# A range clamp moved from VectorE to GpSimd, and a maximum over four written as three elementwise maxima

## The chip, the cores and the metric

The kernel runs on one core of a Trainium2 chip. The core has five engines, each with its own queue of instructions that it takes in order: TensorE (PE; its weight loads are PEld) for matrix products, VectorE (DVE), ScalarE (ACT), GpSimd (POOL), and SyncE (SP), which starts most transfers. They meet only at semaphores. The metric is the device time of one execution in microseconds. Three runs of the kernel before took 1162.79, 1162.80 and 1165.26 us, a median of 1162.8 us.

## The reference, cut to what matters

Three blocks follow each other: an attention with 32 memory slots per head, a dense layer with three weight matrices, and an 8-expert layer in which each expert takes a fixed number of tokens by descending logit.

```python
a = np.exp(phi - np.max(phi, axis=2, keepdims=True))      # phi: 8 x 8 x 576 x 32
a = a / (np.sum(a, axis=2, keepdims=True) + 1e-09)
k_m, v_m = einsum('bhsm,bhsd->bhmd', a, k), einsum('bhsm,bhsd->bhmd', a, v)
attn = softmax((q @ k_m.T) / 8)                            # 8 = sqrt(head_dim)
x = (attn @ v_m) as 4608 tokens x 512
h = np.maximum(np.maximum(x @ w1, x @ w2), x @ w3)         # 512 -> 768
x = h @ w_out                                              # 768 -> 512
logits = x @ w_gate                                        # greedy choice, 576 tokens per expert
out[mask] = np.maximum(x[mask] @ m_w1[e], 0) @ m_w2[e]     # for each expert e
```

The dense weights w1, w2, w3 and w_out arrive as float64. The change touches their conversion to float32 and the maximum over the 576 tokens of phi.

## The kernel before, in words

The eight batches are handled as four units of two. For unit 0 the order of all work is written out as one string of steps, ORDER (lines 30 to 70); later units are interleaved by a planner (Flow) that spreads attention steps between the matrix products of the unit before. In ORDER a name is a step, an exclamation mark continues a step at its next `yield`, and a leading 1 means unit 1. `s0` is the maximum over tokens, `c.0` to `c.11` are the conversions of the layer-1 weights (six column chunks by two row halves), `d.0` to `d.5` those of w_out, `f` folds weights into the attention values, `L` is layer 1 and `s6` the softmax's division.

`s0` (line 270) takes one batch of phi as a tile of 128 partitions, in which a partition holds 4 tokens of each of 8 heads by 32 slots. It reduces the four to one (line 273), adds the remaining 64 tokens by a maximum over 64 partitions (line 276), and TensorE then transposes the result for the maximum over partitions. It runs twice per unit: twice at the start, for unit 1 in lines 35 and 44 of ORDER, and later for units 2 and 3.

`conv` (line 519) turns a float64 tile into float32 by its integer words. ScalarE writes the absolute value of the high word, read as a float32, into the destination (line 529). VectorE clamps that to the range LEAST to MOST (line 532), shifts it by three bits (line 533), brings in the sign (line 535) and the top bits of the low word (line 536). Tiles are 128x768 for the layer-1 weights and 128x512 for w_out. The layer-1 result is also stored to a scratch tensor (line 538), and the next weights are requested. In ORDER `c.n` is the absolute value and `c!.n` all the rest.

GpSimd's own work in the first 160 us is four additions per batch (lines 312 to 315), the softmax's division (line 437), half of the subtractions that split folded weights into a high and a low part (line 586) and the same for w_out (line 547). The low parts feed layer 1 (line 602), whose first matrix product for each chunk and batch half needs them.

Of the kernel before, what the change touches and what calls it, by code (L numbers as in the profile page):

```python
# [12 lines left out]
OP = mybir.AluOpType  # L13
AX = mybir.AxisListType
# [56 lines left out]
LEAST, MOST = 2.0 ** -15, 122879.9921875  # L71
# [71 lines left out]
def moe_kernel(tc, q, k, v, phi, w1, w2, w3, w_out, w_gate, m_w1, m_w2, out):  # L143
    nc = tc.nc
    PE, V, A, G, SP = nc.tensor, nc.vector, nc.scalar, nc.gpsimd, nc.sync
    B, H, S, D = q.shape
# [13 lines left out]
    with ExitStack() as ctx:  # L160
# [106 lines left out]
        def att_steps(u):  # L267
            steps = []

            def s0(b):  # L270
                ph, phr = st["ph", u, b], st["phr", u]
                mt = lp.tile([128, H * M], F32, name="mt", bufs=1)
                V.tensor_reduce(mt.rearrange("p (h m) -> p h m", h=H), ph.rearrange("p h i m -> p h m i"),
                                axis=AX.X, op=OP.max)
                r = slice(64 * b, 64 * b + 64)
                V.tensor_tensor(mt[r], mt[r], phr[r].rearrange("p h m -> p (h m)"), op=OP.max)
                st["mt", u, b] = mt
# [165 lines left out]
            if u < 2:  # L443
                return dict(s0=s0, t0=s0b, s1=s1, t1=s1b, r=s2s, s2=s2, s3=s3, s4=s4, s5=s5, s6=s6)
            add(3.0, P(s0, 0))
            add(3.0, P(s0b, 0), P(s0, 1))
            add(2.0, P(s1, 0), P(s0b, 1))
            add(3.5, P(s1, 1), P(s1b, 0))
# [52 lines left out]
        def load_d(kind):  # L501
            if not todo[kind]:
                return
            x = todo[kind].pop(0)
            if kind == "w":
                i, a = x
                t = xp.tile([128, 2, 384, 2], I32, name="dw", bufs=2)
                for w, src in enumerate((w1, w2, w3)):
                    SP.dma_start(t[:, :, 128 * w:128 * w + 128].rearrange("p j a b -> p j (a b)"),
                                 src.bitcast(I32)[256 * a:256 * a + 256, 256 * i:256 * i + 256].rearrange(  # L510
                                     "(j p) x -> p j x", p=128))
                t = t.rearrange("p j a b -> p (j a) b")
            else:
                t = xp.tile([128, DM, 2], I32, name="do", bufs=1)
                SP.dma_start(t.rearrange("p a b -> p (a b)"), w_out.bitcast(I32)[128 * x:128 * x + 128])
            st["d", kind, x] = t

        @staged
        def conv(kind, *x):
            x = x if len(x) > 1 else x[0]  # L520
            t = st["d", kind, x]
            hi, lo = t[:, :, 1], t[:, :, 0]
            if kind == "w":
                y = st["wr", 0, x[0], x[1]] = ap.tile([128, 2, 384], F32, name="wr", bufs=WR)
                dst = y.rearrange("p j f -> p (j f)")
            else:
                dst = st["wo", x] = wp.tile([128, DM], F32, name="xs", bufs=2)
            e = dst.bitcast(I32)
            A.activation(dst, hi.bitcast(F32), AF.Abs)
            yield  # L530

            V.tensor_scalar(dst, dst, LEAST, MOST, op0=OP.max, op1=OP.min)
            V.tensor_scalar(e, e, 3, 0x3FFFFFFF, op0=OP.logical_shift_left, op1=OP.bitwise_and)

            V.scalar_tensor_tensor(e, hi, -2 ** 30, e, op0=OP.bitwise_and, op1=OP.bitwise_or)
            V.scalar_tensor_tensor(e, lo, 29, e, op0=OP.logical_shift_right, op1=OP.bitwise_or)
            if kind == "w":
                SP.dma_start(ws[x[0], x[1]], dst)
            load_d(kind)
            if kind == "o":  # L540
                yield
                if x == 0:
                    st["wo2"] = [wp.tile([128, NF, 2 * NA], F32R, name=n) for n in ("woh", "wol")]
                woh, wol = st["wo2"]
                A.activation(woh[:, x, :DM], dst, AF.Copy)
                yield
                G.tensor_tensor(wol[:, x, :DM], dst, woh[:, x, :DM].bitcast(F32), op=OP.subtract)
# [603 lines left out]
        for u in range(NU):  # L1151
            if u == 0:
# [10 lines left out]
                for x in ORDER.split():  # L1163
                    name, *x = x.replace("!", "").split(".")
                    x = tuple(int(y) for y in x)
# [135 lines left out]
```

## Time and profile before

| | |
|---|---|
| median of three runs | 1162.8 us |
| profiled execution, its own time | 1156.12 us |
| its span | 1154.3 us |
| TensorE busy | 1067.4 us (92%) |
| VectorE busy | 721.9 us (63%) |
| ScalarE busy | 398.0 us (34%) |
| GpSimd busy | 338.2 us (29%) |
| mean granted TensorE clock | 0.977 |

The profile is one execution with every instruction's start and duration. Busy shares are means over stages with different limits, so the stretches further down are read one by one. Idle time in front of an instruction is listed with what ended it; idle time of an engine that nobody waits for costs nothing. A line number is that of the kernel before, unless an extract of the changed kernel is shown, where lines after 273 stand two further down (line 533 is the clamp there, line 535 the shift).

### The profile page before, as it was taken

The numbers are of one execution on the slowest core, as the hardware profiler recorded it, in microseconds if no ns is written. First come the engines' busy times: TensorE is split into PE (matmuls) and PEld (weight loads), VectorE is DVE, ScalarE is ACT, GpSimd is POOL, SyncE is SP. The second block draws the span as 40 slices with busy tenths as digits, with TensorE's granted clock in tenths as the row PEclk, the third lists the DMA queues.
The fourth block names the chain that finished last, engine by engine and source line by source line (L and its number), as shares of the span: only waits on it lengthen the run. The fifth ranks groups of instructions, "written<-read, shape, count | busy, mean of one in ns | idle before, by whom it ended". The sixth has DMA issues, their size and how long they took to land.

```text
span 1154.3 us, 22040 instructions
## 1 busy us (share of the span) xinstructions
PE 1067.4 (92%) x8743; PEld 931.2 (81%) x8743; DVE 721.9 (63%) x1767; ACT 398.0 (34%) x897; POOL 338.2 (29%) x362
## 2 busy tenths in 40 slices
PE   4698999989999999999997899898999999899996
PEld 3577799878998889778997788778788887879895
DVE  6798843774646446344686577879787887862120
ACT  2454434433343243322332313324142332424240
POOL 2123210120101101000001444555544455556552
PEclk8899999999999999999998989999999999999999
DMA  9964535336322430210132232333313232334311
GB/s 286 324 199 141 183 115 167 108 96 199 104 83 70 138 97 24 74 42 1 47 128 69 83 106 87 110 101 111 114 61 112 82 118 92 121 104 128 106 55 41
DMA packets 103767, 127.80 MB, mean 111 GB/s; under 512 B 18928, under 2 KB 79344, under 8 KB 103664
## 3 DMA queue, kind: packets, MB, share of 16 engines
q1 hardware_dynamic: 95184, 102.80, 28.9%
q0 software_dynamic: 5888, 18.88, 5.2%
q10 hardware_dynamic: 2592, 4.72, 1.1%
q8 instruction: 69, 1.13, 0.4%
q14 instruction: 34, 0.28, 0.1%
HBM read 102.78 MB, written 23.59 MB: 109 GB/s over the span
## 4 chain that ended last, share of the span: by engine, by line
PE 43%; DVE 10%; issue 3%; POOL 2%; ACT 1%; DMA 0%; POOLq 0%
PE acc L1033 13%; PE acc L1010 12%; PE acc L602 5%; PE acc L664 4%; PE acc L1037 2%; PE tr L974 1%; DVE reach L731 1%; PE fold L757 1%; DVE eq L798 1%; PE fold L664 1%; DVE hT L1013 1%; PE fold L743 1%; DVE part L800 1%; POOL bl L995 1%; DVE kn L787 1%
## 5 line engine op out<-in xcount | busy, mean ns | idle before, releaser
L602 PE MATMUL acc<-ah,Wh 128*128 128x288 f32 x576 | 180.1, 313 | 4.9 <-DVE hT L608 3.6
L602 PE MATMUL acc<-ah,Wl 128*128 128x288 f32 x576 | 169.8, 295 | 1.2 <-DVE Wl L586 1.2
L602 PE MATMUL acc<-al,Wh 128*128 128x288 f32 x576 | 169.9, 295 | 0.0
L1033 PE MATMUL acc<-bh,hT 128*128 128x512 f32 x512 | 168.4, 399 | 0.0
L1010 PE MATMUL acc<-woh,ah 128*128 128x288 f32 x512 | 161.0, 314 | 1.7 <-ACT woh L976 1.2
L1010 PE MATMUL acc<-wol,ah 128*128 128x288 f32 x512 | 154.9, 303 | 0.2
L1010 PE MATMUL acc<-woh,al 128*128 128x288 f32 x512 | 154.1, 301 | 0.0
L602 PEld LDWEIGHTS acc<-ah,Wh 128*128 128x128 f32 x576 | 108.2, 188 | 33.3 <-issue 13.9
L608 DVE TENSOR_TENSOR hT<-hT,acc 128x288 f32<-128x288 f32 x192 | 85.9, 450 | 75.1 <-PE acc L602 69.0
L1033 PEld LDWEIGHTS acc<-bh,hT 128*128 128x128 f32 x512 | 96.1, 188 | 21.3
L602 PEld LDWEIGHTS acc<-ah,Wl 128*128 128x128 f32 x576 | 108.2, 188 | 1.4 <-DVE Wl L586 1.4
L602 PEld LDWEIGHTS acc<-al,Wh 128*128 128x128 f32 x576 | 108.4, 188 | 0.1
L985 POOL TENSOR_TENSOR al<-wa,ah 128x512 fp32r<-128x512 f32 x64 | 82.8, 1300 | 72.4 <-ACT ah L984 72.0
L1010 PEld LDWEIGHTS acc<-woh,ah 128*128 128x128 f32 x512 | 99.6, 195 | 3.2 <-ACT woh L976 1.7
L1012 ACT ACTIVATE hT<-acc 128x288 fp32r<-128x288 f32 x128 | 52.6, 411 | 142.4 <-PE acc L1010 136.4
L1033 PE MATMUL acc<-bl,hT 128*128 128x512 f32 x256 | 100.5, 392 | 0.0
L1010 PEld LDWEIGHTS acc<-wol,ah 128*128 128x128 f32 x512 | 99.5, 194 | 1.0 <-DVE wol L977 0.7
L1010 PEld LDWEIGHTS acc<-woh,al 128*128 128x128 f32 x512 | 99.6, 195 | 0.0
L962 POOL DMA_INDIRECT xg<-x2s,gi x40 | 39.3, 982 | 191.9 <-DVE some L751 172.7
L995 POOL TENSOR_TENSOR bl<-wa,bh 128x512 fp32r<-128x512 f32 x64 | 83.6, 1322 | 24.3 <-ACT bh L994 24.0
L1013 DVE SCALAR_TENSOR_TENSOR hT<-acc,hT 128x288 fp32r<-128x288 f32 x128 | 56.2, 452 | 52.4 <-ACT hT L1012 51.7
L606 ACT ACTIVATE hT<-acc 128x288 f32<-128x288 f32 x96 | 38.9, 411 | 144.6 <-PE acc L602 142.6
(253 smaller groups left out, 2204.9 us busy)
## 6 DMA issues: line engine op xcount, KB each, us to landing
wa<-in_moe_w_dram SPq DMA_DIRECT2D x64, 512.0 KB, 3.7
wr<-ws SPq DMA_DIRECT2D x36, 384.0 KB, 3.1
dw<-in_moe_w_dram SPq DMA_DIRECT2D x36, 256.0 KB, 5.3
q<-in_q_dram SPq DMA_DIRECT2D x7, 1024.0 KB, 5.9
kv<-in_k_dram SPq DMA_DIRECT2D x27, 256.0 KB, 4.1
kv<-in_v_dram SPq DMA_DIRECT2D x27, 256.0 KB, 4.9
ws<-wr SPq DMA_DIRECT2D x12, 384.0 KB, 3.1
x2s<-xs ACTq DMA_DIRECT2D x18, 256.0 KB, 2.0
```

What stands on the lines that cost most here:

```text
L602: PE.matmul(p, x[:, b, g, f], y[:, g, c], start=(n == 0), stop=(n == 5))
L606: A.activation(o, p, AF.Copy)
L608: V.tensor_tensor(o, o, p, op=OP.max)
L664: PE.matmul(ps[a], x[:, j], y[:, i, NA * a:NA * a + NA], start=(i == 0 and m == 0), stop=(i == NF - 1 and m == 2))
L962: G.indirect_dma_start(out=x[:n], out_offset=None, in_=x2s, in_offset=bass.IndirectOffsetOnAxis(ap=gi[:n, t:t + 1], axis=0))
L985: G.tensor_tensor(lo, r, hi.bitcast(F32), op=OP.subtract)
L995: G.tensor_tensor(lo, r, hi.bitcast(F32), op=OP.subtract)
L1010: PE.matmul(p, x[:, k], y[:, k, c], start=(k == 0 and i == 0), stop=(k == 3 and i == 2))
L1012: A.activation(hh[:, m, c], p, AF.Relu)
L1013: V.scalar_tensor_tensor(hl[:, m, c], p, 0.0, hh[:, m, c].bitcast(F32), op0=OP.max, op1=OP.subtract)
L1033: PE.matmul(p, x[:, m, c], y[:, m], start=(m == 0 and i == 0), stop=(m == K - 1 and i == 2))
L1037: PE.matmul(p, st["hx", m // 4][:, m % 4], y[:, m], start=(m == 0 and y is bh), stop=(m == K - 1 and y is bl))
```

## The change

The clamp moves to GpSimd and ahead of the `yield`, so that it is issued with the absolute value. The reduction over four tokens becomes three maxima. ORDER is as it was.

```diff
-                V.tensor_reduce(mt.rearrange("p (h m) -> p h m", h=H), ph.rearrange("p h i m -> p h m i"),
-                                axis=AX.X, op=OP.max)
+                x = mt.rearrange("p (h m) -> p h m", h=H)
+                V.tensor_tensor(x, ph[:, :, 0], ph[:, :, 1], op=OP.max)
+                for i in (2, 3):
+                    V.tensor_tensor(x, x, ph[:, :, i], op=OP.max)
...
             A.activation(dst, hi.bitcast(F32), AF.Abs)
+
+            G.tensor_scalar(dst, dst, LEAST, MOST, op0=OP.max, op1=OP.min)
             yield
-
-            V.tensor_scalar(dst, dst, LEAST, MOST, op0=OP.max, op1=OP.min)
             V.tensor_scalar(e, e, 3, 0x3FFFFFFF, op0=OP.logical_shift_left, op1=OP.bitwise_and)
```

GpSimd's queue in the first 100 us, around the seventh and eighth conversion of the layer-1 weights. Before (at is the softmax, Wl a folded weight's low part, wol that of w_out, hh a copy of the folded weight):

```order
L586 TENSOR_TENSOR Wl_628<-hh_646,Wh_627 128x384
L437 TENSOR_TENSOR at_657<-at_657,ssm_708 128x512
L547 TENSOR_TENSOR wol_715<-xs_366,woh_714 128x512
L586 TENSOR_TENSOR Wl_628<-hh_790,Wh_627 128x384
L586 TENSOR_TENSOR Wl_822<-hh_871,Wh_821 128x384
L586 TENSOR_TENSOR Wl_822<-hh_953,Wh_821 128x384
L547 TENSOR_TENSOR wol_715<-xs_775,woh_714 128x512
```

The same place now (wr and xs are the destinations of conversions; L588 is line 586 of before, L439 line 437, L549 line 547):

```order
L533 TENSOR_SCALAR wr_718<-wr_718 128x768
L588 TENSOR_TENSOR Wl_634<-hh_652,Wh_633 128x384
L439 TENSOR_TENSOR at_663<-at_663,ssm_714 128x512
L549 TENSOR_TENSOR wol_722<-xs_371,woh_721 128x512
L533 TENSOR_SCALAR xs_781<-xs_781 128x512
L533 TENSOR_SCALAR wr_823<-wr_823 128x768
L588 TENSOR_TENSOR Wl_634<-hh_797,Wh_633 128x384
L533 TENSOR_SCALAR wr_904<-wr_904 128x768
L588 TENSOR_TENSOR Wl_830<-hh_878,Wh_829 128x384
L588 TENSOR_TENSOR Wl_830<-hh_959,Wh_829 128x384
L549 TENSOR_TENSOR wol_722<-xs_781,woh_721 128x512
```

Four clamps stand between the subtractions and the softmax's division. The eighth conversion (wr_904) has its clamp directly ahead of the subtraction for Wl_830.

VectorE's queue at the same eighth conversion. Before (dw is the loaded float64 tile, hT the result of layer 1, acc and fold are results of TensorE):

```order
L608 TENSOR_TENSOR hT_607<-hT_607,acc_874 128x288
L532 TENSOR_SCALAR wr_897<-wr_897 128x768
L533 TENSOR_SCALAR wr_897<-wr_897 128x768
L535 SCALAR_TENSOR_TENSOR wr_897<-dw_764,wr_897 128x768
L536 SCALAR_TENSOR_TENSOR wr_897<-dw_764,wr_897 128x768
L608 TENSOR_TENSOR hT_607<-hT_607,acc_908 128x288
L586 TENSOR_TENSOR Wl_822<-fold_823,Wh_821 128x384
```

Now (L610 is line 608 of before, L535, L537 and L538 are lines 533, 535 and 536):

```order
L610 TENSOR_TENSOR hT_614<-hT_614,acc_881 128x288
L535 TENSOR_SCALAR wr_904<-wr_904 128x768
L537 SCALAR_TENSOR_TENSOR wr_904<-dw_770,wr_904 128x768
L538 SCALAR_TENSOR_TENSOR wr_904<-dw_770,wr_904 128x768
L610 TENSOR_TENSOR hT_614<-hT_614,acc_915 128x288
L588 TENSOR_TENSOR Wl_830<-fold_831,Wh_829 128x384
```

The clamp is gone from VectorE's queue, and the shift that follows waits for GpSimd in place of ScalarE.

## Rows read from the trace of the kernel before

**Rows 1.** Stretches: us, busy time (instructions) of each engine, granted clock, DMA share, GB/s

```profile
0.00:60.00 60.00, 34.05 (x340) 25.57 (x340) 42.16 (x75) 21.55 (x44) 11.81 (x17) 0.83 1.05 299
60.00:150.00 90.00, 80.61 (x734) 67.80 (x735) 76.62 (x139) 40.72 (x96) 25.33 (x22) 1.00 0.55 177
150.00:330.00 180.00, 175.89 (x1722) 159.00 (x1721) 99.27 (x246) 73.17 (x182) 21.81 (x30) 1.00 0.42 128
330.00:600.00 270.00, 264.08 (x2417) 232.77 (x2416) 143.50 (x361) 90.43 (x225) 11.13 (x13) 1.00 0.21 66
```

**Rows 2.** TensorE in order of time: start, us, instruction [idle before <- releaser]

```profile
47.84 0.66 PE L390 MATMUL tr<-ident,rest 64*128 64x64 f32 x4 [4.39 <-DMA rest<-in_q_dram]
...
60.57 0.65 PE L390 MATMUL tr<-ident,woh 128*128 128x128 f32 x4 [1.01 <-DVE al L493]
...
75.51 0.41 PE L602 MATMUL acc<-ah,Wh 128*128 128x288 f32 x1 [0.91 <-DVE hT L608]
...
80.22 0.40 PE L602 MATMUL acc<-ah,Wh 128*128 128x288 f32 x1
...
89.13 0.87 PE L571 MATMUL fold<-wr,vT 64*32 64x384 f32 x12 [2.48 <-DVE Wl L586]
...
102.34 0.63 PE L619 MATMUL tr<-ident,xs 128*128 128x128 f32 x4 [0.68 <-DVE xs L536]
107.56 0.40 PE L602 MATMUL acc<-ah,Wh 128*128 128x288 f32 x1 [0.40 <-DVE hT L608]
113.92 0.40 PE L602 MATMUL acc<-ah,Wl 128*128 128x288 f32 x1 [1.16 <-DVE Wl L586]
118.44 0.63 PE L619 MATMUL tr<-ident,xs 128*128 128x128 f32 x4 [0.73 <-DVE xs L536]
127.84 0.40 PE L602 MATMUL acc<-ah,Wh 128*128 128x288 f32 x1 [0.71 <-DVE hT L608]
```

**Rows 3.** Groups by line, 0 to 330 us: count | busy us, mean ns | idle before

```profile
L273 DVE TENSOR_REDUCE mt<-ph 128x256 f32<-128x1024 f32 x6 | 11.8, 1962 | 2.0 <-DMA ph<-in_phi_dram 2.0
...
L532 DVE TENSOR_SCALAR wr<-wr 128x768 f32<-128x768 f32 x12 | 7.7, 643 | 1.5 <-ACT wr L529 1.5
...
L532 DVE TENSOR_SCALAR xs<-xs 128x512 f32<-128x512 f32 x6 | 3.3, 548 | 0.0
...
L276 DVE TENSOR_TENSOR mt<-mt,phr 64x256 f32<-64x256 f32 x6 | 2.5, 420 | 0.2
```

**Rows 4.** GpSimd in order of time, two operations with two inputs

```profile
13.53 0.72 POOL L312 TENSOR_TENSOR mt<-ph 128x256 f32<-128x256 f32 x1 [12.43 <-ACT ph L303]
...
75.35 1.02 POOL L586 TENSOR_TENSOR Wl<-hh,Wh 128x384 fp32r<-128x384 f32 x1 [2.66 <-ACT hh L582]
```

**Rows 5.** Line 1020, one input, on GpSimd: duration ns min/median/max, first and last start

```profile
L1020 POOL CAST xs<-hT x32: 389/405/1521, 683.7 to 1131.8; 128x256 fp32r<-128x256 f32 x32
```

**Rows 6.** GpSimd, then VectorE, in order of time near 71 us

```profile
71.08 1.60 POOL L547 TENSOR_TENSOR wol<-xs,woh 128x512 fp32r<-128x512 f32 x1
...
71.57 1.53 DVE L533 TENSOR_SCALAR wr<-wr 128x768 int32<-128x768 int32 x1
```

**Rows 7.** All engines in order of time, 83 to 89 us

```profile
83.31 0.96 DVE L536 SCALAR_TENSOR_TENSOR wr<-dw,wr 128x768 int32<-128x768 int32 x1
83.80 1.35 POOL L586 TENSOR_TENSOR Wl<-hh,Wh 128x384 fp32r<-128x384 f32 x1 [7.43 <-PE acc L602]
...
84.10 0.96 ACT L529 ACTIVATE wr<-dw 128x768 f32<-128x768 f32 x1
...
85.10 0.56 DVE L532 TENSOR_SCALAR wr<-wr 128x768 f32<-128x768 f32 x1 [0.46 <-ACT wr L529]
...
88.52 0.55 DVE L586 TENSOR_TENSOR Wl<-fold,Wh 128x384 fp32r<-128x384 f32 x1
```

**Rows 8.** One stretch of 2 us behind the wait at 47.84 us, columns as in rows 1

```profile
48.00:50.00 2.00, 2.00 (x21) 0.65 (x21) 1.93 (x3) 0.38 (x1) 0.42 (x1) 0.50 1.11 359
```

## Prediction

> **What bounds the kernel now.** I read the stretches first: busy time of each engine, granted clock and DMA share [rows 1]. Then I read TensorE's rows of the first stretches, each with the idle time in front of it and what ended it [rows 2]. Up to 60 us the DMA engines are full (share 1.05) and TensorE works 34.05 of 60 us; its wait at 47.84 us (4.39 us) ends with a load. From 60 to 150 us VectorE is the busiest helper, 76.62 of 90 us, and TensorE works 80.61 us. After 150 us TensorE is busy for 175.89 of 180 us, then 264.08 of 270 us. It takes its instructions in order, so what the first 150 us gain or lose is carried to the end nearly unchanged, and what VectorE is relieved of later is worth almost nothing.
>
> So the change is priced in TensorE's waits between 47.84 and 150 us. Eight of those that VectorE ends carry the sum: 1.01, 0.91, 2.48, 0.68, 0.40, 1.16, 0.73 and 0.71 us [rows 2], 8.1 us together. Before most of them VectorE runs a weight conversion (lines 532 to 536), which the change shortens. 8.1 us is the most that this change can earn there.
>
> **What leaves VectorE.** The clamp, line 532: 12 x 0.643 + 6 x 0.548 = 11.0 us [rows 3]. The reductions of line 273 take 1.962 us each; three maxima of 256 elements stand in for one, eight times in all. The nearest row is line 276, the same operation over 256 elements on half the partitions, 0.420 us [rows 3], so 1.26 us for three and 0.7 us less per step, without the gaps between instructions. From below, a maximum that costs nothing would give 1.96 us; from above, one that takes the 0.64 us of the contended clamp nothing at all. Two of the eight steps stand at the start and the third (line 35 of the order) still ahead of the load at 47.84 us, which takes up what they gain. The fourth (line 44) stands ahead of the wait at 102.34 us and counts. The last four lie where TensorE is full, and I count them as nothing; were TensorE's cover gone there, they would be worth 0.7 us each.
>
> **What GpSimd gets.** Eighteen clamps. No row shows this operation on GpSimd. Two-input rows: 0.72 us for 256 elements, 1.02 for 384 [rows 4]. They give (1.02 - 0.72) / 128 = 2.3 ns per element and 0.12 us fixed; 768 elements would be 1.9 us and 512 1.3 us. The one-input copy of 256 elements has a median of 0.405 us [rows 5]; less 0.12 us that is 1.1 ns per element, so 0.98 us and 0.68 us. The clamp has one input, so I take 0.95 and 0.65 us, 15.3 us in all. The lower bound is the 0.405 us of the copy itself, the upper one 1.9 us.
>
> The Trainium skill (GPSIMD Engine Reference, section 3.1 Elementwise) gives about 2.6 cycles per element for two inputs and 1.03 for a short one-input body at 1.2 GHz; by the second the clamp of 768 would be an estimated 0.66 us and a dispatch. The copy's row agrees with the second figure, and neither moves the sum.
>
> **What the clamps do to VectorE.** Rows show that the two engines exclude each other for some instructions. Line 533 handles the same tile as line 532, which took 0.56 us at 85.10 us [rows 7]. At 71.57 us it began while a GpSimd subtraction ran from 71.08 to 72.68 us, took 1.53 us and ended at 73.10 us, 0.42 us after the other [rows 6]. The other way round, the subtraction at 83.80 us took 1.35 instead of 1.02 us [rows 4], and line 536 ran until 84.27 us beside it [rows 7]. The Trainium skill (GPSIMD Engine Reference, section 1 Specifications) says that this contention hits VectorE instructions in a two-port mode or with two SBUF inputs. These rows agree, and by that rule the new maxima, with two SBUF inputs, can be blocked too, where the old reduction with one could not.
>
> **The places.** In the new order, line 533 of the old numbering waits for the clamp, and the clamp waits on GpSimd's queue behind what stands there and for ScalarE's absolute value. Where the absolute value is early (the second, fourth, seventh and tenth conversion of the layer-1 weights, and most of the w_out ones), VectorE simply loses the clamp: 0.56 to 0.64 us, or 0.55 us. Where it has just ended, VectorE waits longer than its own clamp took, and worse, GpSimd's next queued subtraction starts as soon as the clamp ends and shuts VectorE out again.
>
> The clearest such place is at 85 us. The absolute value ends at 84.10 + 0.96 = 85.06 us, and VectorE has been waiting for it [rows 7]. New: clamp 85.1 to 86.05; then the folded-weight subtraction, ready since 83.80 us, to 87.05; the shift ends 0.42 us later, 87.47 us, instead of 85.10 + 0.56 + 0.59 = 86.25 us. The rest follows unchanged, so the subtraction at 88.52 us begins 1.2 us later and so does TensorE at 89.13 us. Behind the waiting shift stand line 535, line 536, a maximum and that subtraction, and TensorE's fold waits for it.
>
> Going through TensorE's waits in order (differences to now, in us):
> - 60.57: the conversion ahead has its clamp early, -0.6 of the 1.01.
> - 75.51: given back, +0.6. The sixth conversion of the layer-1 weights has its clamp ahead of the last attention rows on GpSimd, and three subtractions alternate with VectorE's conversion.
> - 89.13: +1.2 as above.
> - 102.34: -0.68; the w_out conversion ahead loses its clamp, and the fourth maximum step gives 0.6 more than is needed.
> - 107.56: +0.3, again an absolute value that ends just in time with a subtraction queued behind the clamp.
> - 113.92: -0.6; 118.44: -0.7; 127.84: -0.6, where a queued subtraction falls into a gap of VectorE.
>
> Sum: -0.6 + 0.6 + 1.2 - 0.7 + 0.3 - 0.6 - 0.7 - 0.6 = -1.1 us. GpSimd's folded weights come up to 3 us later behind the clamps. What hides that: the one that ends at 75.35 + 1.02 = 76.37 us is first read after 80.22 us [rows 4, 2]. If that cover were gone, TensorE would wait for GpSimd directly.
>
> The profiled execution took 1156.1 us, a span of 1154.3 us and 1.8 us around it, and would take 1155.0 us. It lies 6.7 us under the median of the runs, 1162.8 us. The difference of 1.1 us is carried over: **1161.7 us**.
>
> **Rivals.**
> *The relief passes through whole.* VectorE is 85% busy between 60 and 150 us, which speaks for it. Each wait shrinks by what the conversions ahead of it lose: 0.6 + 0.6 + 1.7 (three conversions ahead of the 2.48) + 0.6 + 0.4 + 0.6 + 0.55 + 0.6 = 5.6 us, so 1157.2 us. Against it: where the two engines meet, GpSimd's time comes back as VectorE's [rows 6, 7].
>
> *GpSimd's queue becomes the bound (slower).* The place is the one at 85 us. If the clamp costs the two-input 1.9 us, each of three late places (89.13, 107.56, 127.84) loses 0.95 us more: -1.1 + 2.9 = +1.8 us. The wait at 89.13 us then reaches 2.48 + 1.2 + 0.95 = 4.6 us, longer than the 4.39 us at 47.84 us, after which the granted clock stood at 0.50, the 1.2 GHz level [rows 8, 2]. Were that to hold for the 5 us of a few such stretches (my estimate), it would cost 2.5 us: +4.3, so 1167.1 us. It decides from a clamp of about 0.95 + 1.1 / 3 = 1.3 us on. Against it: the clamp has one input, as the copy.
>
> *Nothing to see.* The gains fall on waits that ScalarE or a load ends next, and the losses on slack: 1162.8 us. For it: the waits are short, and what ends each is only the last of several that are due.
>
> **Chances and range.** Forecast 0.47 (its own range 1159.5 to 1164.0 us), whole relief 0.23, GpSimd's queue 0.18, nothing 0.12. Under 0.2% (2.3 us) a measurement of this kernel tells no change. Faster by more: 0.23 and a quarter of the forecast's, 0.35. Slower by more: 0.18, and 0.04 from the edges of the others, 0.22. Within: 0.43. The range from 1157.2 to 1166.0 us leaves out about half of each outer rival.
>
> **What would show it.** In the profile after: GpSimd's clamp near 0.95 us for 768 elements (1.3 us or more speaks for the slower rival); three maxima of 0.42 us in place of 2.0; VectorE's busy time down by about 11 us for the clamps, and the first shift longer than 0.56 us where a GpSimd subtraction runs. TensorE's wait near 89 us should grow and those after 100 us shrink; the wait at 47.84 us should end at the same time. I am wrong if the wait near 89 us shrinks, if TensorE waits for GpSimd's folded weights, or if something after 150 us moves by over 1 us.

## The result and the profile after

The changed kernel takes 1179.08 us (median of 4 runs, 1174.15 to 1179.93); the kernel before, run beside it, takes 1163.18 us. The ratio is 1.0124, with a 95% interval of 1.0094 to 1.0155: slower by some 14 us (10.9 to 18.0 us by the interval; the medians differ by 15.9 us). The forecast was 1161.7 us and its range ended at 1166.0 us.

The profiled execution after took 1174.15 us, a span of 1172.4 us. It is the fastest of the four and has the highest mean granted clock, 0.983 against 0.966, 0.966 and 0.976, so the others can hold more of the low clock than is shown below. Its stretches, in the columns of [rows 1]:

```profile
0.00:60.00 60.00, 34.43 (x340) 25.31 (x340) 39.73 (x77) 20.76 (x43) 24.87 (x22) 0.94 1.01 292
60.00:150.00 90.00, 70.90 (x603) 59.07 (x604) 66.39 (x110) 37.98 (x88) 52.98 (x32) 0.96 0.51 161
150.00:330.00 180.00, 175.84 (x1740) 157.91 (x1738) 97.67 (x250) 70.53 (x173) 25.16 (x33) 1.00 0.44 130
330.00:600.00 270.00, 265.29 (x2443) 233.60 (x2436) 140.18 (x345) 93.10 (x229) 12.85 (x15) 1.00 0.20 63
```

Read them against [rows 1]. Up to 60 us TensorE has done the same 340 matmul records. From 60 to 150 us it does 603 where it did 734, and is busy for 70.90 us where it was busy for 80.61. VectorE is less busy, 66.39 us instead of 76.62, and GpSimd twice as busy, 52.98 instead of 25.33. The loss lies in this stretch; after it TensorE is as full as before.

The groups of the edited lines, 0 to 330 us, in the columns of [rows 3] (with what ended the idle time). Old lines behind 273 stand two lower, so the clamp is line 533 and VectorE's shift line 535:

```profile
L533 POOL TENSOR_SCALAR wr<-wr 128x768 f32<-128x768 f32 x12 | 34.4, 2870 | 32.0 <-ACT wr L531 31.4 <-PE acc L604 0.6
L533 POOL TENSOR_SCALAR xs<-xs 128x512 f32<-128x512 f32 x6 | 11.5, 1924 | 8.9 <-ACT xs L531 8.9
...
L535 DVE TENSOR_SCALAR wr<-wr 128x768 int32<-128x768 int32 x12 | 12.6, 1047 | 17.8 <-POOL wr L533 17.8
...
L276 DVE TENSOR_TENSOR mt<-mt,ph 128x256 f32<-128x256 f32 x12 | 5.4, 448 | 0.4
...
L274 DVE TENSOR_TENSOR mt<-ph 128x256 f32<-128x256 f32 x6 | 2.5, 420 | 0.7 <-DMA ph<-in_phi_dram 0.7
```

The maxima are what was forecast: 0.42 to 0.45 us each, 1.3 us for three in place of 1.96 us. The clamp is not. On GpSimd it has a median of 2.77 us for 768 elements (mean 2.87) and 1.92 us for 512, where VectorE took 0.64 and 0.55 us [rows 3], and VectorE's shift now waits for it, 17.8 us in all.

The place that the prediction worked through, all engines in order of time (the shift of the eighth conversion, [rows 7] of before):

```profile
90.56 0.95 ACT L531 ACTIVATE wr<-dw 128x768 f32<-128x768 f32 x1
...
91.60 2.77 POOL L533 TENSOR_SCALAR wr<-wr 128x768 f32<-128x768 f32 x1 [4.33 <-ACT wr L531]
...
94.33 0.99 POOL L588 TENSOR_TENSOR Wl<-hh,Wh 128x384 fp32r<-128x384 f32 x1
94.40 1.34 DVE L535 TENSOR_SCALAR wr<-wr 128x768 int32<-128x768 int32 x1 [4.36 <-POOL wr L533]
...
98.01 0.55 DVE L588 TENSOR_TENSOR Wl<-fold,Wh 128x384 fp32r<-128x384 f32 x1
...
98.61 1.52 PE L573 MATMUL fold<-wr,vT 64*32 64x384 f32 x12 [5.51 <-DVE Wl L588]
```

The absolute value ends at 91.51 us, the clamp runs to 94.37, then GpSimd's queued subtraction to 95.32, and VectorE's shift, which began beside it, ends at 95.74: 0.42 us after the subtraction, exactly the exclusion of [rows 6]. TensorE's wait of 2.48 us [rows 2] has become 5.51 us.

TensorE's waits of the first 200 us after the change (us in total, times, longest):

```profile
PE fold L573 <- DVE Wl L588: 8.6, 3, 5.5
PE tr L286 <- DVE mt L278: 8.3, 2, 7.0
PE tr L480 <- POOL at L439: 6.2, 3, 3.2
PE tr L325 <- POOL mt L317: 4.8, 2, 4.4
PE acc L604 <- DVE hT L610: 3.8, 2, 2.9
PE tr L392 <- DVE ssm L437: 3.0, 1, 3.0
```

and before:

```profile
PE tr L284 <- DVE mt L276: 9.4, 2, 7.7
PE tr L390 <- DMA rest<-in_q_dram: 4.4, 1, 4.4
PE fold L571 <- DVE Wl L586: 3.6, 2, 2.5
PE tr L323 <- POOL mt L315: 3.1, 2, 2.4
PE acc L602 <- DVE hT L608: 2.0, 3, 0.9
```

The wait for the folded weights' low part has grown from 3.6 to 8.6 us. The 6.2 us for the softmax on GpSimd (at, line 439) are new. GpSimd at that place, in order of time:

```profile
62.19 2.77 POOL L533 TENSOR_SCALAR wr<-wr 128x768 f32<-128x768 f32 x1 [6.10 <-ACT wr L531]
64.93 1.04 POOL L439 TENSOR_TENSOR at<-at,ssm 64x512 f32<-64x512 f32 x1
69.61 1.05 POOL L439 TENSOR_TENSOR at<-at,ssm 128x512 f32<-128x512 f32 x1 [3.64 <-DVE ssm L437]
```

The division at 64.93 us starts the moment the clamp ends. The one at 69.61 us waited for VectorE's row sum (ssm), which stands on VectorE behind a shift that waits for the same clamp: GpSimd is named as the releaser, but the chain goes back to the clamp both ways.

Two stretches of the changed kernel show TensorE's granted clock at its lower level of 1.2 GHz (columns as in rows 1); before, it stood at 1.00 from 60 to 600 us [rows 1]:

```profile
72.00:74.00 2.00, 2.00 (x10) 1.98 (x10) 1.66 (x5) 1.50 (x3) 0.94 (x1) 0.50 0.51 173
...
100.00:102.00 2.00, 2.00 (x16) 1.93 (x10) 0.05 (x1) 1.25 (x3) 0.48 (x1) 0.58 1.01 299
```

The low clock runs from 70.9 to 74.4 us and from 98.3 to 101.7 us, each time from the end of a wait on (3.25 us up to 70.72 us, 5.51 us up to 98.61 us). Of some 7 us at half speed about 3.5 us are lost (my estimate: half of the time, since TensorE is busy in nearly all of it).

The loss in order of time, as the shift of one and the same instruction (matching instructions of TensorE, after minus before, us), beside the running sum of the prediction:

| place (before) | forecast, running sum | measured shift |
|---|---|---|
| 60.57 | -0.6 | -0.2 |
| 75.51 | 0.0 | +5.8 |
| 89.13 | +1.2 | +9.5 |
| 102.34 | +0.5 | +9.9 |
| 107.56 | +0.8 | +12.7 |
| 113.92 | +0.2 | +12.9 |
| 118.44 | -0.5 | +12.0 |
| 127.84 | -1.1 | +14.0 |

The row that answers to the one at 113.92 us in [rows 2] is this one of TensorE:

```profile
126.84 0.40 PE L604 MATMUL acc<-ah,Wl 128*128 128x288 f32 x1 [1.37 <-DVE Wl L588]
```

From 138 to 230 us the shift stays at 13.9 us. This shift is the cleanest measure in the traces and is used below as "the shift at 140 us". It is that of one execution: two kernels below whose instructions are the same up to 57 us (the maxima alone and the one place) stand at -1.0 and -0.5 us there. At 609 us, where the part with the experts begins, the shift is 11.9 us. From that point to the end identical instructions take 545.3 us in the trace before and 554.5 us in that of the maxima alone, so the ends of two single profiles can't be compared to better than some 9 us; the timed ratios can.

### The profile page after: what moved, and what is told of

It reads as the page before. It is cut to its first block, busy times and chain, and to the rows that moved or that the text cites. A ratio compares the mean times of both kernels' runs of the same rounds, so it can differ in the third digit from the quotient of the medians.

```text
span 1172.4 us, 22061 instructions
## 1 busy us (share of the span) xinstructions
PE 1070.3 (91%) x8743; PEld 931.4 (79%) x8743; DVE 712.5 (61%) x1765; ACT 398.5 (34%) x897; POOL 383.7 (33%) x380
## 4 chain that ended last, share of the span: by engine, by line
PE 41%; DVE 11%; issue 3%; POOL 2%; ACT 1%; DMA 0%; POOLq 0%
PE acc L1035 13%; PE acc L1012 10%; PE acc L604 5%; PE acc L666 4%; PE acc L1039 2%; DVE reach L733 2%; PE tr L976 1%; PE fold L759 1%; DVE eq L800 1%; PE fold L666 1%; DVE hT L1015 1%; PE fold L745 1%; DVE part L802 1%; POOL bl L997 1%; DVE kn L789 1%
## 5 line engine op out<-in xcount | busy, mean ns | idle before, releaser
L610 DVE TENSOR_TENSOR hT<-hT,acc 128x288 f32<-128x288 f32 x192 | 85.9, 450 | 79.6 <-PE acc L604 71.6
L1047 POOL DMA_INDIRECT out_dram<-o,si x40 | 47.6, 1191 | 142.1 <-ACT o L1043 88.9
L997 POOL TENSOR_TENSOR bl<-wa,bh 128x512 fp32r<-128x512 f32 x64 | 83.7, 1331 | 22.5 <-ACT bh L996 22.2
L1043 ACT ACTIVATE o<-acc 128x512 f32<-128x512 f32 (+1 forms) x40 | 23.9, 598 | 190.9 <-PE acc L1035 138.3
```

The lines of the kernel that those rows point to most:

```text
L610: V.tensor_tensor(o, o, p, op=OP.max)
L997: G.tensor_tensor(lo, r, hi.bitcast(F32), op=OP.subtract)
L1043: A.activation(o[:n], p[:n], AF.Copy)
L1047: s = G.indirect_dma_start(out=out, out_offset=bass.IndirectOffsetOnAxis(ap=st["si", ph][:n, t:t + 1], axis=0), in_=o[:n], in_offset=None)
```

## The experiments

Four theories: **A**, VectorE waits behind clamps on GpSimd whose input is only just there, at 2.77 us each. **B**, GpSimd's busy time as such costs, by sharing with VectorE and by delaying GpSimd's other work. **C**, the maxima cost. **D**, the clamp's place ahead of the yield blocks GpSimd's queue behind ScalarE. A diff is against the kernel before; "+ maxima" means that the first diff is in the kernel too.

**The maxima alone** (C).

```
-  V.tensor_reduce(mt..., axis=AX.X, op=OP.max)
+  V.tensor_tensor(x, ph[:, :, 0], ph[:, :, 1], op=OP.max)
+  for i in (2, 3):
+      V.tensor_tensor(x, x, ph[:, :, i], op=OP.max)
```

> The three maxima alone; the clamp stays on VectorE. Theory A (VectorE and GpSimd's queue stand still behind a clamp that costs 2.77 us): the maxima have no part in the loss; 0 to 3 us faster than before, since only the step at about 93 us has TensorE waiting behind VectorE. Theory C (the maxima with their two inputs are what loses, by being shut out): 5 us slower or more.

Measured: 1.0007 (0.9989 to 1.0026), no change clear of noise (-1.3 to +3.0 us). C falls. The trace shows a loss and a gain. The loss is at TensorE's wait near 89 us and in the stretches behind it:

```profile
88.08 0.87 PE L573 MATMUL fold<-wr,vT 64*32 64x384 f32 x12 [2.49 <-DVE Wl L588]
```

```profile
88.00:90.00 2.00, 1.93 (x20) 1.30 (x20) 0.02 (x1) 1.01 (x3) 0.00 (x0) 0.92 0.95 270
90.00:92.00 2.00, 2.00 (x12) 2.00 (x11) 0.92 (x2) 0.25 (x1) 1.68 (x2) 0.50 0.97 323
92.00:94.00 2.00, 2.00 (x11) 2.00 (x10) 0.02 (x1) 1.29 (x4) 0.55 (x1) 0.50 0.00 0
```

Up to here this execution is 1.05 us ahead of the one before. Then, behind a wait of the same length, 2.49 us, the clock stands at 0.50 from 89.7 to 96.5 us, and from 113 us on it is 1.5 us behind. That this loss is the maxima's is not shown: of the seven traces in which this wait is 2.47 to 2.49 us long, the clock falls behind it in two.

The gain comes after 230 us, where the prediction counted the last four maximum steps as nothing. From 230 to 609 us the shift falls from 1.5 to -0.6 us here, from 13.9 to 11.9 us in the changed kernel, and by 1.7 to 2.6 us in eleven of the twelve traces with the maxima; in the twelfth (the late eight below) a low clock at 275 us covers it. In the only trace without them, the clamps alone, it does not fall (16.6 to 18.1 us, with a low clock at 276 us). It falls at and behind the four steps, which stood at 232, 236, 358 and 364 us before. Two of TensorE's waits from 150 to 600 us shrink (us in total, times, longest), before:

```profile
PE sc L344 <- DMA kv<-in_v_dram: 2.9, 2, 2.1
PE acc L602 <- DVE hT L608: 1.6, 3, 1.0
```

with the maxima alone:

```profile
PE sc L346 <- DMA kv<-in_v_dram: 1.2, 1, 1.2
PE acc L604 <- DVE hT L610: 1.0, 1, 1.0
```

and with the clamps alone they stay:

```profile
PE sc L344 <- DMA kv<-in_v_dram: 2.7, 2, 1.9
PE acc L602 <- DVE hT L608: 1.6, 3, 1.0
```

So the maxima are worth some 2 us there, which the timed runs are too coarse to show.

**The clamps alone**, without the maxima.

```
-  yield
-  V.tensor_scalar(dst, dst, LEAST, MOST, op0=OP.max, op1=OP.min)
+  G.tensor_scalar(dst, dst, LEAST, MOST, op0=OP.max, op1=OP.min)
+  yield
```

> The clamp alone on GpSimd; the reduction stays. Theory A: the whole loss is here, 14 to 18 us slower than before, about 1 us more than the changed kernel. Theory C: under 5 us slower.

Measured: 1.0136 (1.0102 to 1.0170), 15.8 us. The whole loss is the clamps'. In this trace the clock is low for 20.5 us between 60 and 150 us, where the changed kernel's had 6.8 us, and the shift at 140 us is 16.6 us.

**The clamps beside** (A against B): GpSimd clamps a scratch tile that nobody reads; VectorE keeps its own clamps, + maxima.

```
+  scratch = xp.tile([128, 768], F32, name="scratch"); G.memset(scratch, 1.0)
...
+  z = scratch[:, :dst.shape[1]]
+  G.tensor_scalar(z, z, LEAST, MOST, op0=OP.max, op1=OP.min)
   yield
   V.tensor_scalar(dst, dst, LEAST, MOST, op0=OP.max, op1=OP.min)
```

> Maxima, clamp on VectorE as before, and in addition the same 18 operations on GpSimd at the same places in its queue, on a tile of their own that nobody reads: GpSimd is as busy, but nobody waits for the clamp and it does not wait for ScalarE. Theory A (waiting): at most 4 us slower than before, what is left being GpSimd's own later rows that are late. Theory B (the two engines' shared access, whoever waits): most of the loss stays, 8 us slower or more, with VectorE's conversion rows stretched.

Measured: 1.0078 (1.0050 to 1.0107), 9.0 us, which is theory B's case by the time (5.8 to 12.4 us leaves out A's 4 us). VectorE's shift (line 539 here, 533 before) by groups, in the columns of [rows 3], beside the clamps and before:

```profile
L539 DVE TENSOR_SCALAR wr<-wr 128x768 int32<-128x768 int32 x12 | 9.6, 802 | 0.4
```

```profile
L533 DVE TENSOR_SCALAR wr<-wr 128x768 int32<-128x768 int32 x12 | 8.4, 698 | 0.4
```

The instructions beside the clamps are stretched by some 0.1 us each and VectorE never waits for GpSimd's clamps. The shift at 140 us is 4.1 us, 2.6 more than with the maxima alone. So B is real, but this trace shows only a part of the 9 us.

**The scratch tile without the clamps** asks whether the rest comes from the tile, which moves what lies behind it; + maxima.

```
+  scratch = xp.tile([128, 768], F32, name="scratch"); G.memset(scratch, 1.0)
```

> Maxima as in the change, all clamps on VectorE as before, and the scratch tile of 128x768 with one fill on GpSimd, but no clamp on it: the run with clamps beside, less its clamps. That run took 9.0 us more than before, of which its trace shows 4.2 us up to 230 us. If the rest comes from GpSimd's clamps (theory B), this one takes as long as the maxima alone, -1 to +2 us. If it comes from the tile that was added, which moves what is placed behind it in memory, this one is 3 to 7 us slower than before, and the clamps beside cost 2 to 5 us by sharing, no more.

Measured: 0.9998 (0.9975 to 1.0021). The tile costs nothing that these runs can tell (-2.9 to +2.4 us); the clamps beside do cost 6 to 12 us by the interval. The execution with clamps beside whose trace was read is the fastest of its five, 1165.94 us, 2.8 us over the median of the kernel before, near its shift of 2.5 us at 609 us. The part beyond that lies in the other four executions (1169.48 to 1175.87 us), which have no trace. The mean granted clock of the five is 0.968 to 0.973, that of the kernel before beside them 0.970 to 0.983: this points to the clock, but does not show it.

**One operation instead of two** (price): the clamp on GpSimd applies only the maximum, the upper limit is left out, + maxima.

```
+  G.tensor_scalar(dst, dst, LEAST, None, op0=OP.max)
```

> The changed kernel with the maximum only, without the minimum, in the clamp (the upper end of the range is left out). If the price goes with the number of operations, the row falls from 2.77 to about 1.5 us and Theory A has the loss fall to 3 to 7 us. If the price goes with the elements alone, the row stays at 2.8 us and the loss at 14 to 18 us. Theory B: the loss falls in proportion to GpSimd's busy time, to about half.

Measured: 1.0104 (1.0074 to 1.0134), 12.1 us, between the cases of the expectation. The clamp's group:

```profile
L533 POOL TENSOR_SCALAR wr<-wr 128x768 f32<-128x768 f32 x12 | 27.2, 2269 | 35.3 <-ACT wr L531 34.4 <-PE acc L604 0.9
```

The median falls from 2.77 to 2.13 us, by 0.64 us, and the shift at 140 us from 13.9 to 9.7 us, by 4.2 us. Eight late places at 0.64 us would be 5.1 us. So a second operation costs 0.64 us and not, as the first case had it, half of the clamp. The ratios alone don't separate the two kernels (their intervals overlap); the price is read from the traces.

**No clamp at all** (what the relief of VectorE is worth): the range limit is left out, + maxima.

```
-  V.tensor_scalar(dst, dst, LEAST, MOST, op0=OP.max, op1=OP.min)
```

> Maxima, and no clamp on any engine (the range limit is left out): VectorE is relieved of 11 us and nobody is charged. What the whole relief would be worth at best: the prediction's rival sized it at 5.6 us, so 4 to 7 us faster than before if that holds. If the relief ends in waits for something else, under 2 us faster.

Measured: 0.9957 (0.9940 to 0.9975), 5.0 us faster. In size that is the prediction's whole relief of 5.6 us, but in part by chance: in the trace the shift is -3.3 us at 140 us, where the 5.6 us should all have been earned, and -5.5 us at 609 us, so 2.2 us of it are the maxima's later steps. A low clock behind the wait near 89 us, only 1.87 us long here, took back 2.5 us (shift -2.7 us ahead of it, -0.2 us at 93 us). The best version that keeps the clamp, below, gained 1.7 us.

**The late and the early clamps apart**, + maxima. Where a clamp isn't sent to GpSimd it stays on VectorE. The condition is all that differs (conversions of the layer-1 weights are counted from 0; kind "o" is w_out). In these kernels the clamp on GpSimd is line 535 and VectorE's shift line 539:

```
+  if early: G.tensor_scalar(dst, dst, LEAST, MOST, op0=OP.max, op1=OP.min)
   yield
+  if not early: V.tensor_scalar(dst, dst, LEAST, MOST, op0=OP.max, op1=OP.min)
w_out only:  early = kind == "o"
early ones:  early = kind == "o" or 2 * x[0] + x[1] in (1, 3, 6, 9)
late eight:  early = kind == "w" and 2 * x[0] + x[1] not in (1, 3, 6, 9)
one place:   early = kind == "w" and x == (3, 1)
early five:  early = kind == "o" or 2 * x[0] + x[1] in (1, 3, 6, 9, 11)
```

> Maxima, and only the six w_out clamps on GpSimd; the twelve of the layer-1 weights stay on VectorE. Theory A (waiting behind late clamps): the w_out values come early, so nobody waits; within 1.5 us of before. Theory B (GpSimd's busy time as such): 11.5 us more of it, a quarter of the 46 us of the kernel with the operations beside, so 1.5 to 2 us slower.

> Maxima, the six w_out clamps and the four of the second, fourth, seventh and tenth layer-1 conversion on GpSimd, which the prediction counted as early; eight stay on VectorE. Theory A: 2 us faster to 2 us slower than before. Theory B: 22.6 us more of GpSimd, 3 to 4 us slower.

> Maxima as in the change; of the clamps only the eight layer-1 conversions whose absolute value ends just in time (the first, third, fifth, sixth, eighth, ninth, eleventh and twelfth) run on GpSimd, 8 x 2.77 = 22.2 us there instead of 45.9; the other ten stay on VectorE. Theory A (VectorE waits behind late clamps): the complement of these on GpSimd cost nothing (-1.6 us), the whole change +15.9 us by the runs so far, so these eight carry it all: +14 to +19 us, and VectorE shows six or more waits for GpSimd's clamp of 12 us or more together in the first 170 us. Theory B (GpSimd's busy time and its shared access as such): the cost goes with the time on GpSimd, 22.2 / 45.9 of 16 us, +6 to +9 us.

Measured: w_out only 0.9992 (0.9975 to 1.0010); the ten early ones 0.9985 (0.9971 to 0.9999), 1.7 us faster (0.1 to 3.4 us), the best version that keeps the clamp; the eight late ones 1.0141 (1.0107 to 1.0174), 16.3 us slower. VectorE's wait for GpSimd's clamps of the layer-1 weights in the first 170 us, with the early ones:

```profile
DVE wr L539 <- POOL wr L535: 0.5, 1, 0.5
```

and with the late eight:

```profile
DVE wr L539 <- POOL wr L535: 16.0, 7, 4.0
```

The two parts add up: -1.7 + 16.3 = 14.6 us, and the whole change costs 14.4 us. Both parts contain the maxima, which change little (0.8 us by the ratio, -1.3 to +3.0). The 1.7 us can be the maxima's alone, so the early clamps are shown to cost nothing, not to gain. The late eight spend about half of the clamps' time on GpSimd and carry all of the loss, as A says and B does not. How much of their 16.3 us B adds to the waits is not separated: by its time on GpSimd, 22.2 of 45.9 us, it would be some 4 of the 9.0 us of the clamps beside (my estimate).

> Maxima as in the change; one single clamp runs on GpSimd, that of the eighth layer-1 conversion, whose absolute value ends at 85.06 us just when VectorE waits for it. Theory A, worked out with the measured price of 2.77 us: clamp 85.1 to 87.9 us, the queued subtraction of 1.0 us to 88.9 us, the shift 0.42 us behind it at 89.3 us instead of 86.25 us, so TensorE's wait of 2.48 us near 89 us grows by 3.0 us (2.7 to 3.4); all in all +1.5 to +3 us, since part of it may be taken up by the short waits that follow. With the 0.95 us that was forecast for a clamp it would be 1.2 us. Theory B (busy time as such): 2.77 of 45.9 us, +1.0 us at the most, and the wait near 89 us grows by no more than 1 us.

Measured: 1.0040 (1.0027 to 1.0052), 4.6 us for a single clamp, more than A's 1.5 to 3 us. The place, in order of time:

```profile
84.64 2.79 POOL L535 TENSOR_SCALAR wr<-wr 128x768 f32<-128x768 f32 x1 [8.75 <-PE acc L608]
...
87.41 0.98 POOL L592 TENSOR_TENSOR Wl<-hh,Wh 128x384 fp32r<-128x384 f32 x1
87.46 1.36 DVE L539 TENSOR_SCALAR wr<-wr 128x768 int32<-128x768 int32 x1 [3.33 <-POOL wr L535]
...
91.69 1.52 PE L577 MATMUL fold<-wr,vT 64*32 64x384 f32 x12 [5.54 <-DVE Wl L592]
```

TensorE's wait grows from 2.48 to 5.54 us, by 3.06 us; 3.0 was worked out. The rest is the clock, which stands at 0.50 behind it (columns as in rows 1):

```profile
92.00:94.00 2.00, 2.00 (x15) 0.86 (x4) 0.00 (x0) 0.73 (x2) 0.00 (x0) 0.50 0.98 287
94.00:96.00 2.00, 2.00 (x11) 2.00 (x10) 0.92 (x2) 0.52 (x2) 1.40 (x2) 0.50 0.69 237
96.00:98.00 2.00, 2.00 (x11) 2.00 (x11) 0.00 (x0) 0.56 (x3) 0.82 (x1) 0.50 0.00 0
98.00:100.00 2.00, 2.00 (x10) 2.00 (x10) 1.09 (x3) 0.72 (x4) 0.00 (x0) 0.50 0.04 8
```

The shift, -0.5 us ahead of the wait, is 2.6 us at its end and 6.3 us at 113 us: 3.1 us from the wait and 3.8 us behind it, while TensorE ran at half speed. Up to 230 us none of it is absorbed. The expectation missed by this: it had no term for the clock and had the short waits take up a part. The fall to 3.7 us at 609 us is that of the maxima.

> Maxima as in the change; on GpSimd the six clamps of w_out and those of the layer-1 conversions whose absolute value is early, five of the twelve (second, fourth, seventh, tenth, and also the twelfth), the other seven stay on VectorE. Theory A: VectorE loses 11 clamps of 0.55 to 0.64 us and waits for hardly one: 1 to 3 us faster than before; if the twelfth is a late one, it costs 1 to 2.8 us and the kernel comes out between 1.5 us faster and 1.5 us slower. Theory B: 25.4 of 45.9 us of clamps on GpSimd, 4 to 9 us slower.

Measured: 1.0020 (1.0008 to 1.0033), 2.3 us slower (0.9 to 3.8 us; the expectation had at most 1.5). The fifth, the twelfth conversion, is a late one after all. GpSimd's clamp, and VectorE's shift:

```profile
120.90 2.77 POOL L535 TENSOR_SCALAR wr<-wr 128x768 f32<-128x768 f32 x1 [3.26 <-ACT wr L531]
```

```profile
123.70 1.64 DVE L539 TENSOR_SCALAR wr<-wr 128x768 int32<-128x768 int32 x1 [1.80 <-POOL wr L535]
```

The shift at 140 us is +1.8 us, against -1.2 us with the four: 3.0 us for this one clamp, with a stretch of low clock in it (129.1 to 132.5 us) that the run with the four does not have.

**The clamp behind the yield** (D): it then stands on GpSimd where it stood on VectorE, + maxima.

```
   yield
+  G.tensor_scalar(dst, dst, LEAST, MOST, op0=OP.max, op1=OP.min)
```

> The changed kernel with the clamp behind the yield, directly ahead of the shift: GpSimd's queue no longer stands behind ScalarE's absolute value early, but all 18 shifts now wait for a whole clamp. Theory A: 12 x 2.2 + 6 x 1.4 = 35 us more on VectorE than with its own clamps, some of it hidden: 20 to 35 us slower than before. Theory D (the loss comes from GpSimd's queue standing behind ScalarE): the loss shrinks, under 10 us slower.

Measured: 1.0238 (1.0209 to 1.0266), 27.6 us slower, in A's range. VectorE's wait for the clamp (line 534; the shift is line 535):

```profile
DVE wr L535 <- POOL wr L534: 32.0, 7, 8.1
```

D falls as the main cause: the early place in the queue softens the loss.

## Why the prediction was wrong

**The step that failed is the price of the clamp**: "The clamp has one input, so I take 0.95 and 0.65 us", with 1.9 us as the upper bound. Measured: 2.77 and 1.92 us, and the bound itself was passed. The copy's 0.405 us [rows 5] was taken as the nearest row because it has one input; the clamp costs even more than the two-input line through [rows 4], with one operation (2.13 us) as with two. The trace of before held no row of this operation on GpSimd, and the two lines that I drew from its neighbours did not enclose it. The Trainium skill (GPSIMD Engine Reference, section 3.1 Elementwise) led the same way: its 1.03 cycles per element for a short body would be an estimated 0.66 us. The runs show 2.77 us, and the measurement decides.

**The mechanism was the slower rival's.** It said that GpSimd's queue becomes the bound from 1.3 us on, at the place near 85 us, and that the wait at 89 us would then pass the one at 47.84 us and bring the clock down. All three are in the rows above. That a wait has to be longer than the one at 47.84 us for this is not borne out: the clock also fell behind 2.49 us and 1.87 us. Put the measured price into the prediction's own working of that place and it gives +3.0 us; the run with that clamp alone shows +3.06 us.

**The size of that rival was short by a factor of about two.** By its own rule, three places and 2.77 in place of 0.95 us, it is -1.1 + 3 x 1.82 = +4.4 us, and +6.9 us with the 2.5 us for the clock. The shift at 140 us is 13.9 us. The count of places is what lacked: the prediction had three, and at 2.77 us every one is late whose absolute value ends less than 2.77 us before VectorE wants it. In the trace before these leads are, for the first to the twelfth conversion, 0.0, 2.4, 0.8, 3.0, 1.6, 1.5, 5.1, 0.0, 1.6, 4.2, 1.3 and 1.1 us. Nine of the twelve are too short; the second lacks only 0.4 us (it is the wait of 0.5 us of the run with the early ones), and the run with the other eight alone loses as much as the whole change. By the table, the step to 75.51 us alone is +6.0 us where the sum had +0.6 (there lie the softmax on GpSimd and the first low clock), and the three from 113.92 to 127.84 us make +1.3 us together where it had -1.9. The clock took about 3.5 us in this execution where 2.5 were estimated.

**A second step failed the other way.** The last four maximum steps "lie where TensorE is full, and I count them as nothing". They are worth some 2 us between 230 and 609 us (13.9 to 11.9 us), most of the 2.8 us that four steps of 0.7 us would be without that cover.

**What was right.** The maxima's size: 0.42 us each. The early clamps: VectorE hardly waits for them, and the ten together cost nothing. The whole relief: 5.6 us worked out, 5.0 us measured without the clamp, but by luck in part, since 2.2 us of it came from places that the 5.6 us did not count. The exclusion of the two engines, to the 0.42 us. And the cover up to 60 us: the shift there is -0.2 us.

**What was said to show it wrong** did, in one of its three forms: after 150 us something moves by more than 1 us (the maxima's 2 us, and not the clamps). TensorE does not wait for GpSimd's folded weights; it waits for GpSimd's softmax, which the prediction did not have.

**Not settled:** the clamps beside cost 6 to 12 us in the timed runs and about 4 us in the one trace up to 230 us. The effect of GpSimd's work where nobody waits for it is therefore known in its sum only. It isn't known either why a wait of 2.49 us is followed by the low clock in the kernel with the maxima alone, and one of 2.48 us before by none, nor how much of the timed 14.4 us is the clock: the execution whose trace was read has the highest granted clock of the four.

## What to carry to other kernels

Work that moves to a slower engine is priced by the lead: where its input is there early the busy engine does not pay, and where it comes just in time the whole of the slower engine's duration stands in the chain, so sort the instances by lead first and move only the early ones. Do not take "the engine behind is full" for a price of nothing without looking at its remaining waits. If no row of the trace shows the operation on its new engine, let the range reach to where the sign turns, however well a neighbouring operation seems to fit. And ask how many places become late at the upper price, not only how much later the known ones get.

## What the runs showed of the hardware

- On GpSimd a tensor_scalar of f32 with two operations took 2.77 us for 128x768 and 1.92 us for 128x512, that is 3.3 ns per element of a partition and 0.2 us fixed; with one operation 2.13 and 1.49 us, 2.5 ns. The one-input copy took 0.405 us for 256 [rows 5] and the two-input subtraction 1.02 us for 384 [rows 4].
- A clamp of 2.77 us on GpSimd beside VectorE's instructions stretches these by about 0.1 us in the mean, while a subtraction on GpSimd held VectorE's shift until 0.42 us after its own end.
- The granted clock fell to 0.50 behind a wait of TensorE of 2.48 or 2.49 us in two traces (the tile alone, the maxima alone), stayed at 1.00 behind one of 2.47 or 2.48 us in five others ([rows 2] is one), and fell behind one of 1.87 us without the clamps. Around a wait of 5.5 us it was low in all five traces that have one: for 3.4 us (the change), 6.8 us (the clamp behind the yield) and 10.2 us (the clamps alone, the late eight, the one place). The length of the wait alone tells neither whether it falls nor how long it stays low.
